# Order of the DMA transposes of q and k for two batches, in a fused sliding-window attention and GEGLU kernel

## The chip, the cores and the metric

The kernel runs on one core of a Trainium2 chip. The metric is the device time of one execution in microseconds (us). The kernel before has a median of 341.93 us over 3 runs (341.65 to 343.43). TensorE is called PE, VectorE DVE, ScalarE ACT, GpSimd POOL and SyncE SP. SP computes nothing here: it issues DMAs.

## The reference

Eight batches of attention with 8 heads, 576 positions and head size 64. Each query sees the 128 positions up to and including itself, with a bias that falls with distance (ALiBi). The result, as 4608 rows of 512, goes through a gated feed-forward block.

```python
scores = scale * np.matmul(q, k.transpose(0, 1, 3, 2))
mask = (rel >= 0) & (rel < window)                  # window = 128
scores = np.where(mask, scores + bias[None], -1000000000.0)
attn = softmax(scores)
x = np.matmul(attn, v)                              # heads side by side: 4608 x 512
out = (gelu(x @ w_gate) * (x @ w_val)) @ w_out      # 512 -> 1536 -> 512
```

## The kernel before

The work is written out by hand: the order of the instructions in the source is the order on each engine, and the framework adds only the semaphores. The outer loop `for g in range(NG)` (L909) runs over nine groups of 512 rows. Each group does the feed-forward block of its rows (`gate_val`, L597, with matmuls at L612; `out_part`, L641, with matmuls at L648) and, in between, pieces of the attention of a later batch. The list `todo` (L886) and the function `steps` (L891) say which pieces: in group 0, the scores of batch 1 and its products with v; in group 1, the scores of batch 2 ("s"), its products ("pv+"), and the scores of batch 3 ("s2"); in group 2, the products of batch 3 ("pv") and the scores of batch 4, and so on.

From batch 2 on, q and k of a batch come in like this. GpSimd issues ten loads, five of q and then five of k (`load_qk`, L112), which also turn float32 into bfloat16; five of v follow (`load_v`, L116). They land in buffers `qs`, `ks`, `vb`, two of each, used by even and odd batches in turn. Then `transposes_dma` (L169) makes SP issue six DMA transposes: one for all of k, into `kT` (L170), and five for q, one per block of 128 rows, into `qT` (L174). The scores need both: the matmuls at L206 (batches 0 to 2) and at L288 (from batch 3 on, `scores2`).

An engine takes its instructions in order, and an instruction that waits for a semaphore holds all that stand behind it. On SP the transposes stand in one line with the stores of the output (L638) and with small relays (L199), by which in `scores2` one row group of matmuls lets another begin. For batches 1 and 2 the relays of the products are on DVE instead. The transposes of batch 2 stand in the list of group 0; those of the later batches are issued when the next group starts (L910).

When GpSimd may start the loads of a later batch is ruled by marks: tiny copies on GpSimd that read an element which some earlier step writes, so that GpSimd waits for it. The mark at L952, at the end of group 0, reads `kT[0]`, so it waits for the k transpose of batch 2; then come the loads of q and k of batch 3 and of v of batch 2. The mark at L914, at the start of group 1, reads columns 128 and 129 of `qT[1]`, so it waits for the second q transpose of batch 3; then come the loads of q and k of batch 4 and of v of batch 3. The later marks (L936) read a result of the feed-forward block.

From batch 3 on the row sums are inverted and spread over the partitions by DMAs that ACT issues (`gather`, L435, and `spread_dma`, L443, with L445 filling `rb`), and DVE multiplies the products by them (L547). For batch 2 ACT does the inversion itself (L520, L521) and DVE multiplies at L524. ACT and DVE also copy the output from PSUM (L653), and ACT makes exp (L219) and gelu (L618). [...] a matmul can also wait for a bank to be read out.

Of the kernel before, what the change touches and what calls it, by code (L numbers as in the profile page):

```python
# [30 lines left out]
def kernel(  # L31
# [10 lines left out]
    nc = tc.nc  # L42
# [27 lines left out]
    def keep_busy(ps, n, w=64):  # L70
        for _ in range(n):
# [18 lines left out]
    mark = consts.tile([1, 2], BF16, name="mark")  # L90

    qs, ks = ([consts.tile([128, 5, DM], BF16, name=f"{nm}s{i}") for i in range(2)]
              for nm in "qk")
    qT, kT = ([consts.tile([128, 4, 640], BF16, name=f"{nm}T{i}") for i in range(2)]
              for nm in "qk")
# [16 lines left out]
    def load_qk(b):  # L112
        load(qs[b % 2], q, b)
        load(ks[b % 2], k, b)

    def load_v(b, js=range(5)):  # L116
        load(vb[b % 2], v, b, js, 64)
# [44 lines left out]
    def transpose(b, what, c, copy):  # L162
        ps = bank().bitcast(BF16)
        for n, lo in ((0, 0), (1, 384)):
            transpose_runs(b, n, what, c, ps[:, lo:576])
        for n, lo in ((0, 0), (1, 384)):
            untangle(copy, b, n, what, c, c + 1, ps[:, lo:576])

    def transposes_dma(b):  # L169
        nc.sync.dma_start_transpose(  # L170
            out=kT[b % 2].rearrange("p c (j t) -> p (c j) t", t=128),
            in_=ks[b % 2].rearrange("p j x -> p (j x)"))
        for j in range(5):
            nc.sync.dma_start_transpose(  # L174
                out=qT[b % 2][:, :, 128 * j:128 * j + 128], in_=qs[b % 2][:, j, :])


    Ps = [consts.tile([128, H, 896], BF16, name=f"P{i}") for i in range(2)]
# [188 lines left out]
    def add(b, c0, copy=None, what=(0, 1)):  # L367
        hs = slice(2 * c0, 2 * c0 + 4)
        P = Ps[b % 2].rearrange("p h (n y) -> p h n y", y=64)[:, hs]
        to = T.rearrange("p h (n y) -> p h n y", y=64)[:, hs]  # L370
        if 0 in what:
            for x in (0, 1):
                half = slice(64 * x, 64 * x + 64)
                nc.vector.tensor_tensor(  # L374
                    out=to[half, :, x:x + 7:2], in0=P[half, :, 0:10:3], in1=P[half, :, 1:11:3],
                    op=ALU.add)
            nc.vector.tensor_copy(out=to[0:64, :, 8], in_=P[0:64, :, 12])
            nc.vector.tensor_tensor(
                out=to[64:128, :, 8], in0=P[64:128, :, 11], in1=P[64:128, :, 12], op=ALU.add)
        if 1 in what:  # L380
            for x in (0, 1):
                half, n = slice(64 * x, 64 * x + 64), 4 - x
                (copy or nc.vector.tensor_copy)(
                    out=to[half, :, x + 1:x + 2 * n:2], in_=P[half, :, 2:3 * n:3])
# [30 lines left out]
    def sums4(b):  # L415
        ps = bank()
        for s, at in ((0, 0), (1, shape(b, 0)[1])):
            first, w = shape(b, s)
            mms = []
            for h in range(H):  # L420
                for x in (0, 1):
                    t = first + w * x
                    g, a = 2 * x + h // 4, 32 * (h % 4)
                    mms.append((g, ones8[:, a:a + 32], T[:, h, t:t + w]))
            for n, (g, lhsT, rhs) in enumerate(in_turn(mms)):
                nc.tensor.matmul(  # L426
                    out=ps[32 * g:32 * g + 32, at:at + w], lhsT=lhsT, rhs=rhs,
                    start=n < 4 and s == 0, stop=True, skip_group_check=True)
        for s, at in ((0, 0), (1, shape(b, 0)[1])):
            first, w = shape(b, s)  # L430
            nc.vector.reciprocal(row(b)[:, first:first + w], ps[:, at:at + w])  # L431
# [165 lines left out]
    def gate_val(g, f, lo=0, hi=512, later=None):  # L597
        if g not in hid:
            hid[g] = h_pool.tile([128, NF, 512], BF16, name="hT")
        t0 = 512 * g % RING  # L600
        n = hi - lo

        if n > 256 or lo >= 384:
            pg, pv = bank()[:, 0:n], bank()[:, 0:n]
            order = [(w, ps, c, c == 0) for w, ps in ((wg, pg), (wv, pv)) for c in range(4)]
        else:
            ps = bank()
            pg, pv = ps[:, 0:n], ps[:, n:2 * n]
            order = [(w, ps, c, w is wg and c == 0)
                     for cs in ((0, 1), (2, 3)) for w, ps in ((wg, pg), (wv, pv)) for c in cs]  # L610
        for w, ps, c, begins in order:
            nc.tensor.matmul(  # L612
                out=ps, lhsT=w[:, c, 128 * f:128 * (f + 1)], rhs=xT[:, c, t0 + lo:t0 + hi],
                start=begins, stop=(c == 3), skip_group_check=n <= 256 and lo < 384)

        def act():
            gl = g_pool.tile([128, 512], BF16, name="gelu")
            nc.scalar.activation(out=gl[:, 0:n], in_=pg, func=AF.Gelu)  # L618
            nc.vector.tensor_tensor(out=hid[g][:, f, lo:hi], in0=pv, in1=gl[:, 0:n],  # L619
                                    op=ALU.mult)  # L620

        if later is None:
            act()
        else:
            later.append(act)
# [79 lines left out]
    for h in (0, 2, 4, 6):  # L705
        for w, src in ((0, q), (1, k)):
            (nc.scalar if w and h == 0 else nc.sync).dma_start(
                out=raw[w][h // 4].rearrange("p (h x) -> p h x", h=4)[:, h % 4:h % 4 + 2, :],
                in_=src[0][h:h + 2, 0:384, :].rearrange("h (p r) d -> p h (r d)", r=3))
# [42 lines left out]
    def masks_of_last_blocks(lo, hi):  # L752
        nc.vector.tensor_copy(out=emask[:, lo:hi, 192:384], in_=emask[:, lo:hi, 0:192])
        nc.vector.tensor_copy(out=emask[:, lo:hi, 384:512], in_=emask[:, lo:hi, 0:128])
        for x, at in ((0, 128), (1, 0)):
            half = slice(64 * x, 64 * x + 64)
            nc.vector.tensor_copy(out=emask[half, lo:hi, 512:576], in_=emask[half, lo:hi, at:at + 64])
# [63 lines left out]
    for step in zip(*(inverse_first(0, x, sums_a[x]) for x in (0, 1))):  # L821
        for do in step:
            do()
    dve(out=pairs1.rearrange("p x (h d) -> p h x d", d=64),
        in_=vb[1].rearrange("p j x -> p (j x)")[:, 0:1536].rearrange(
            "p (h x d) -> p h x d", h=H, x=3))
# [6 lines left out]
    masks, waiting = [], []  # L833
# [38 lines left out]
    for n in range(2):  # L872
        nc.gpsimd.dma_start(
            out=wo[:, 6 * n:6 * n + 6, :],
            in_=moe_w_out[768 * n:768 * n + 768, :].rearrange("(c p) f -> p c f", p=128))
# [4 lines left out]
    for t in (qs[0], ks[0]):  # L880
# [3 lines left out]

    acts = (act, act, act, act)
    todo = {  # L886
        0: [("table",), ("s", 1, 0, (0, 1)), ("o", 0, 0, 0), ("o", 0, 1, 0), ("s", 1, 0, (2, 3)), ("o", 0, 0, 1), ("s", 1, 1, (0, 1)), ("o", 0, 1, 1), ("s", 1, 1, (2, 3), masks), ("pv+", 1, 0), 4, ("pv+", 1, 1), ("transposes", 2), 4],
        1: [("table",), ("s", 2, 0, (0, 1)), 3, ("s", 2, 0, (2, 3)), 2, ("s", 2, 1, (0, 1)), 2, ("s", 2, 1, (2, 3), masks), ("pv+", 2, 0), 3, ("pv+", 2, 1), 1, 2, ("s2", 3, 0), ("add", 3, 0), 3, ("s2", 3, 2), ("add", 3, 2, None, (0,))],
    }

# [18 lines left out]
    for g in range(NG):  # L909
        if 1 <= g < B - 2:  # L910
            transposes_dma(3 if g == 1 else g + 2)
        if g == 1:

            nc.gpsimd.tensor_copy(out=mark, in_=qT[1][0:1, 0, 128:130])  # L914
            load_qk(4)
            load_v(3)
        for f in range(9 if g == 0 else 0, NF):
            gate_val(g, f)
            if g == 2 and f == 2:
                add(3, 2, act, (1,))  # L920
            if g == 0 and f == 10:
                masks_of_last_blocks(0, 8)
            if g == 0 and f in (9, 11):
                for c in (0, 1) if f == 9 else (2, 3):
                    for w in (0, 1):
                        transpose(1, w, c, (act, dve)[w])
            if 2 <= g < B - 1:
                if f == (4 if g == 2 else 3):
                    sums4(g + 1)
                if f == (6 if g == 2 else 5):  # L930
                    gather(g + 1)
                if f == (8 if g == 2 else 7):
                    spread_dma(g + 1)
                if f == 9 and g + 2 < B:

                    nc.gpsimd.tensor_copy(out=mark, in_=hid[g][0:1, f, 0:2])  # L936
                    if g + 3 < B:
                        load_qk(g + 3)
                    load_v(g + 2)
        if g == 0:  # L940
            nc.gpsimd.memset(Ps[0][:, :, 0:64], 0.0)
            for t in (qs[1], ks[1]):
                nc.gpsimd.memset(t[64:128, 4, :], 0.0)
        for item in steps(g):
            if isinstance(item, int):
                out_part(g, item)
            else:
                RUN[item[0]](*item[1:])
        store()
        if g == 0:  # L950

            nc.gpsimd.tensor_copy(out=mark, in_=kT[0][0:1, 0, 512:514])  # L952
            load_qk(3)
            load_v(2)

# [29 lines left out]
```

## Time and profile before

| What | Value |
|---|---|
| Median of 3 runs | 341.93 us (341.65 to 343.43) |
| Profiled execution: its own time | 342.81 us |
| Profiled execution: its span | 341.0 us |
| Granted TensorE clock, mean | 0.998 |
| SP issues batch 2's k transpose, then its five q transposes | from 58.91 for 3.18 us, from 62.14 for 6.61 us |
| SP issues batch 3's k transpose, then its five q transposes | from 80.35 for 4.00 us, from 84.40 for 7.29 us |
| Mark L952 runs | at 64.10 us |
| Mark L914 runs | at 89.81 us |
| First scores of batch 2, of batch 3 | at 79.09 us, at 93.58 us |

Times inside the execution are counted from the start of the span. The span is shorter than the execution's own time, which has start and end around it. The profile comes from one execution; the median comes from others. PE's records are of pipelined matmuls with modelled ends, so a gap on PE is what counts, not its busy time. A line number in the profile is that of the kernel before.

### The profile page before, as it was taken

How to read it: one execution, taken by the hardware profiler on the slowest of the kernel's cores; microseconds unless marked ns; L12 is line 12 of the kernel's file. 1: busy time of each engine (PE TensorE's matmuls, PEld its weight loads, DVE VectorE, ACT ScalarE, POOL GpSimd, SP SyncE). 2: the span in 40 equal slices, each digit the busy share in tenths (PEclk: the TensorE clock that was granted, in tenths of full speed). 3: DMA queues.
4: the chain of work that ended last, by engine and by line, in shares of the span. 5: the costliest groups of instructions: out<-in, count | busy, mean ns of one | idle time of the engine just before them, and what ended most of it. 6: DMA issues, size and time to landing. Idle time of an engine off the chain costs nothing.

```text
span 341.0 us, 8148 instructions
## 1 busy us (share of the span) xinstructions
PE 329.0 (96%) x3299; PEld 169.9 (50%) x3342; DVE 192.5 (56%) x358; ACT 172.3 (51%) x321; POOL 106.4 (31%) x142
## 2 busy tenths in 40 slices
PE   8999999999979999999999999999999999999996
PEld 6667555444544454445544454445444544444443
DVE  7888766445659547943695369635974323303320
ACT  7974597438878328433763357344823133223321
POOL 6975763481481086007700680040000000000000
PEclk9999999999999999999999999999999999999999
DMA  8999999999999799949993999399106110020002
GB/s 211 169 193 191 204 164 146 139 184 163 98 207 187 108 173 189 199 110 152 178 190 81 163 179 195 73 161 111 63 3 140 63 62 1 2 93 31 2 31 92
DMA packets 150026, 43.49 MB, mean 128 GB/s; under 512 B 133572, under 2 KB 142948, under 8 KB 149988
## 3 DMA queue, kind: packets, MB, share of 16 engines
q0 software_dynamic: 107424, 18.10, 69.9%
q1 hardware_dynamic: 39104, 18.55, 22.9%
q10 hardware_dynamic: 3460, 6.32, 8.7%
q8 instruction: 26, 0.43, 0.5%
q14 instruction: 12, 0.10, 0.1%
HBM read 43.65 MB, written 9.53 MB: 156 GB/s over the span
## 4 chain that ended last, share of the span: by engine, by line
PE 71%; DMA 16%; POOL 4%; SPq 3%; DVE 2%; issue 2%; ACT 0%; ACTq 0%; DVEq 0%; POOLq 0%
PE ps L612 44%; PE ps L648 20%; DMA ks<-in_k_dram 6%; DMA wo<-in_moe_w_out_dram 5%; DMA rb<-rd 3%; PE ps L490 3%; PE ps L288 2%; POOL qs L108 2%; POOL ks L108 2%; SPq L174 2%; DMA qT<-qs 2%; DMA kT<-ks 2%; SPq L170 1%; PE ps L426 1%; PE ps L682 1%
## 5 line engine op out<-in xcount | busy, mean ns | idle before, releaser
L619 DVE TENSOR_TENSOR hT<-ps,gelu 128x512 bf16<-128x512 f32 (+3 forms) x119 | 73.9, 636 | 93.0 <-PE ps L612 85.3
L618 ACT ACTIVATE gelu<-ps 128x512 bf16<-128x512 f32 (+3 forms) x119 | 65.4, 558 | 101.1 <-PE ps L612 96.8
L612 PE MATMUL ps<-xT,wv 128*128 128x512 bf16 (+3 forms) x472 | 112.9, 359 | 0.5 <-DMA wv<-in_moe_w_val_dram 0.2
L612 PE MATMUL ps<-xT,wg 128*128 128x512 bf16 (+3 forms) x461 | 111.9, 359 | 1.1 <-issue 0.4
L648 PE MATMUL ps<-wo,hT 128*128 128x512 bf16 x375 | 87.8, 379 | 2.0 <-issue 1.1
L612 PEld LDWEIGHTS <-wv 128*128 128x128 bf16 x476 | 45.3, 98 | 49.2 <-issue 0.5
L612 PEld LDWEIGHTS <-wg 128*128 128x128 bf16 x476 | 44.7, 98 | 48.0 <-issue 0.3
L648 PEld LDWEIGHTS <-hT 128*128 128x128 bf16 x396 | 37.0, 98 | 43.8
L219 ACT ACTIVATE P<-ps 128x512 bf16<-128x512 f32 (+1 forms) x108 | 51.3, 578 | 4.5 <-PE ps L288 2.9
L222 DVE TENSOR_TENSOR P<-P,emask 128x768 bf16<-128x768 bf16 x60 | 31.3, 556 | 19.7 <-ACT P L219 18.0
L653 ACT COPY osb<-ps 128x512 f32<-128x512 f32 x28 | 16.4, 587 | 50.8 <-PE ps L648 50.8
L108 POOL DMA_DIRECT2D vb<-in_v_dram x40 | 33.9, 872 | 8.6 <-DMA qs<-in_q_dram 2.5
L108 POOL DMA_DIRECT2D qs<-in_q_dram x30 | 25.3, 861 | 6.0 <-DMA wo<-in_moe_w_out_dram 4.2
L936 POOL COPY mark<-hT 1x2 bf16<-1x2 bf16 x4 | 0.7, 176 | 81.4 <-DVE hT L619 81.4
L108 POOL DMA_DIRECT2D ks<-in_k_dram x30 | 25.4, 887 | 0.3 <-DMA qs<-in_q_dram 0.3
L547 DVE TENSOR_TENSOR xT<-ps,rb 128x512 bf16<-128x512 f32 (+3 forms) x34 | 14.6, 501 | 7.2 <-PE ps L490 4.8
L490 PE MATMUL ps<-P,vb 64*64 64x192 bf16 (+2 forms) x752 | 16.9, 220 | 0.2
L490 PEld LDWEIGHTS <-vb 64*64 64x64 bf16 x752 | 14.4, 107 | 3.1 <-issue 2.6
L374 DVE TENSOR_TENSOR T<-P 64x1024 bf16<-64x1024 bf16 x20 | 13.7, 686 | 0.6
L288 PE MATMUL ps<-qT,kT 64*64 64x192 bf16 (+2 forms) x440 | 9.6, 224 | 2.5 <-DMA qT<-qs 1.9
L288 PEld LDWEIGHTS <-kT 64*64 64x64 bf16 x440 | 7.6, 107 | 7.4 <-issue 7.2
L431 DVE RECIPROCAL r<-ps 128x128 f32<-128x128 f32 (+1 forms) x10 | 9.8, 1021 | 0.0
(92 smaller groups left out, 184.3 us busy)
## 6 DMA issues: line engine op xcount, KB each, us to landing
out_dram<-osb SPq DMA_DIRECT2D x35, 256.0 KB
rb<-rd ACTq DMA_DIRECT2D x10, 576.0 KB
vb<-in_v_dram POOLq DMA_DIRECT2D x32, 128.0 KB, 6.8
qs<-in_q_dram POOLq DMA_DIRECT2D x24, 128.0 KB, 5.7
ks<-in_k_dram POOLq DMA_DIRECT2D x24, 128.0 KB, 6.9
wo<-in_moe_w_out_dram POOLq DMA_DIRECT2D x2, 768.0 KB, 14.7
wg<-in_moe_w_gate_dram POOLq DMA_DIRECT2D x5, 256.0 KB, 8.5
wv<-in_moe_w_val_dram POOLq DMA_DIRECT2D x5, 256.0 KB, 9.1
```

What stands on the lines that cost most here:

```text
L108: nc.gpsimd.dma_start(out=t[at:at + n, j, :].rearrange("p (h d) -> p h d", h=H), in_=src[b][:, 128 * j:128 * j + n, :].rearrange("h p d -> ...
L219: nc.scalar.activation(out=dst, in_=src, func=AF.Exp, scale=0.125)
L222: nc.vector.tensor_tensor(out=dst, in0=dst, in1=m, op=ALU.mult)
L288: mm = nc.tensor.matmul(out=ps[64 * x:64 * x + 64, col:col + w], lhsT=keys(b, c, m)[half, :], rhs=qT[b % 2][half, c, q0:q0 + w], start=Tru ...
L374: nc.vector.tensor_tensor(out=to[half, :, x:x + 7:2], in0=P[half, :, 0:10:3], in1=P[half, :, 1:11:3], op=ALU.add)
L490: mm = nc.tensor.matmul(out=out, lhsT=lhsT, rhs=prob(b)[half, c, i, col:col + q1 - q0], start=all(t[2] != u for t in todo[:n]), stop=True, ...
L547: nc.vector.tensor_tensor(out=xT[:, c, at:at + e - a], in0=src, in1=recip[b][:, c, a:e], op=ALU.mult)
L612: nc.tensor.matmul(out=ps, lhsT=w[:, c, 128 * f:128 * (f + 1)], rhs=xT[:, c, t0 + lo:t0 + hi], start=begins, stop=(c == 3), skip_group_che ...
L618: nc.scalar.activation(out=gl[:, 0:n], in_=pg, func=AF.Gelu)
L619: nc.vector.tensor_tensor(out=hid[g][:, f, lo:hi], in0=pv, in1=gl[:, 0:n], op=ALU.mult)
L648: nc.tensor.matmul(out=acc[g], lhsT=hid[g][:, f, 128 * t:128 * (t + 1)], rhs=wo[:, f, :], start=(f == 0), stop=(f == NF - 1))
L653: (nc.vector.tensor_copy if g < B - 2 and t in by_dve.get(g, (0,)) else nc.scalar.copy)(out=osb, in_=acc[g])
```

## The change

Three edits. First, `transposes_dma` issues the five q transposes ahead of the k transpose for batches 2 and 3; from batch 4 on the order stays k, then q. Second, the entry of batch 2's transposes in the list of group 0 stands ahead of the second half of batch 1's products instead of behind it. Third, the two marks read other elements: that of L952 the last block of `qT[0]`, which the last of the five q transposes of batch 2 writes; that of L914 a column of `kT[1]`, which the k transpose of batch 3, now the last of six, writes.

```diff
     def transposes_dma(b):
-        nc.sync.dma_start_transpose(
-            out=kT[b % 2].rearrange("p c (j t) -> p (c j) t", t=128),
-            in_=ks[b % 2].rearrange("p j x -> p (j x)"))
+        def of_k():
+            nc.sync.dma_start_transpose(
+                out=kT[b % 2].rearrange("p c (j t) -> p (c j) t", t=128),
+                in_=ks[b % 2].rearrange("p j x -> p (j x)"))
+
+        if b > 3:
+            of_k()
         for j in range(5):
             nc.sync.dma_start_transpose(
                 out=qT[b % 2][:, :, 128 * j:128 * j + 128], in_=qs[b % 2][:, j, :])
+        if b <= 3:
+            of_k()
...
-        0: [... ("pv+", 1, 0), 4, ("pv+", 1, 1), ("transposes", 2), 4],
+        0: [... ("pv+", 1, 0), 4, ("transposes", 2), ("pv+", 1, 1), 4],
...
         if g == 1:
 
-            nc.gpsimd.tensor_copy(out=mark, in_=qT[1][0:1, 0, 128:130])
+            nc.gpsimd.tensor_copy(out=mark, in_=kT[1][0:1, 0, 512:514])
             load_qk(4)
             load_v(3)
...
         if g == 0:
 
-            nc.gpsimd.tensor_copy(out=mark, in_=kT[0][0:1, 0, 512:514])
+            nc.gpsimd.tensor_copy(out=mark, in_=qT[0][0:1, 0, 512:514])
             load_qk(3)
             load_v(2)
```

More of the change, by code (lines that the diff above doesn't have):

```diff
@@ L886 @@
     todo = {
-        0: [("table",), ("s", 1, 0, (0, 1)), ("o", 0, 0, 0), ("o", 0, 1, 0), ("s", 1, 0, (2, 3)), ("o", 0, 0, 1), ("s", 1, 1, (0, 1)), ("o", 0, 1, 1), ("s", 1, 1, (2, 3), masks), ("pv+", 1, 0), 4, ("pv+", 1, 1), ("transposes", 2), 4],
+        0: [("table",), ("s", 1, 0, (0, 1)), ("o", 0, 0, 0), ("o", 0, 1, 0), ("s", 1, 0, (2, 3)), ("o", 0, 0, 1), ("s", 1, 1, (0, 1)), ("o", 0, 1, 1), ("s", 1, 1, (2, 3), masks), ("pv+", 1, 0), 4, ("transposes", 2), ("pv+", 1, 1), 4],
         1: [("table",), ("s", 2, 0, (0, 1)), 3, ("s", 2, 0, (2, 3)), 2, ("s", 2, 1, (0, 1)), 2, ("s", 2, 1, (2, 3), masks), ("pv+", 2, 0), 3, ("pv+", 2, 1), 1, 2, ("s2", 3, 0), ("add", 3, 0), 3, ("s2", 3, 2), ("add", 3, 2, None, (0,))],
```

## The prediction

> **What bounds the kernel now.** I read the page's first two parts, the list of waits of PE, the chain of waits that ended last, the timeline around PE's longest gap, and the DMA queues slice by slice.
>
> ```profile
> PE 329.0 (96%) x3299; PEld 169.9 (50%) x3342; DVE 192.5 (56%) x358; ACT 172.3 (51%) x321; POOL 106.4 (31%) x142
> ```
>
> TensorE (PE) is busy 329.0 of 341.0 us at a granted clock of 0.998. Only its gaps, 12 us in all, can be won. PE's waits, longest first (total, times, longest):
>
> ```profile
> PE ps L288 <- DMA qT<-qs: 1.9, 1, 1.9
> PE ps L648 <- issue: 1.1, 7, 0.2
> PE ps L72 <- DVE zeros L696: 1.0, 1, 1.0
> PE ps L288 <- DVE xT L547: 0.6, 2, 0.3
> ```
>
> Two concern the change. The longest is the scores of batch 3 (L288) waiting for a transposed q. The 0.6 is a later wait for the DVE multiply L547, which itself waited for a DMA (rb<-rd). The chain of waits shows where both come from (start, length, what):
>
> ```profile
> 52.24 6.47 DMA ks<-in_k_dram
> ...
> 58.91 5.14 DMA kT<-ks
> ...
> 64.10 0.18 POOL mark L952
> ...
> 71.96 8.18 DMA ks<-in_k_dram
> ...
> 80.35 4.00 SPq L170
> ...
> 84.40 1.26 SPq L174
> ...
> 87.08 1.99 SPq L174
> ...
> 90.48 5.24 DMA qT<-qs
> ...
> 95.76 0.81 PE ps L288 x27
> ...
> 115.66 0.66 ACTq L445
> ...
> 116.36 10.36 DMA rb<-rd
> ...
> 126.84 2.49 DVE xT L547 x4
> ```
>
> Read downwards: batch 2's k lands at 58.7, its transpose lands at 64.05 and lets mark L952 go; batch 3's loads start; its k lands at 80.19; SP issues the k transpose (4.00) and only then five q transposes (7.29 with the gaps), though q had landed long before; the last q lands at 95.72. PE had been ready since 93.58:
>
> ```profile
> 91.79 2.65 SPq L638 DMA_DIRECT2D out_dram<-osb  x3
> 92.98 1.55 DVE L524 TENSOR_TENSOR xT<-ps,rb 128x512 bf16<-128x512 f32 x3
> 93.38 0.57 ACT L653 COPY osb<-ps 128x512 f32<-128x512 f32 x1
> 93.58 0.28 PE L288 MATMUL ps<-qT,kT 64*64 64x64 bf16 x4
> 95.76 0.84 PE L288 MATMUL ps<-qT,kT 64*64 64x192 bf16 x40 [1.90 <-DMA qT<-qs]
> ```
>
> What loads and transposes do to each other is seen in the queues (q0: GpSimd's loads, q1: SP's stores and transposes; packets, MB, share). First pair: half a microsecond from 67.0, both at work. Then loads alone, 78 to 80, and transposes alone, 61 to 62.
>
> ```profile
> q0 software_dynamic: 212, 0.03, 82.3%
> q1 hardware_dynamic: 203, 0.05, 78.7%
> ...
> q0 software_dynamic: 2445, 0.31, 241.5%
> ...
> q1 hardware_dynamic: 839, 0.21, 117.1%
> ```
>
> Alone, loads move some 611 packets per half microsecond and transposes 420; together 212 and 203.
>
> [...] So a transpose that waits at the head of SP's stream holds all behind it, as the 24.6 us that SP spent at L170 waiting for k show. [...]
>
> **The change, part by part.**
>
> *Batch 2's entry moved up* past ("pv+", 1, 1). Nothing that this entry issues goes to SP (its relays are on DVE, its stores are issued by the output parts), so on SP, PE, ACT, DVE and GpSimd every instruction keeps its place. 0 us.
>
> *Batch 2, q ahead of k.* The five q transposes no longer stand behind the wait for k (58.91). SP is free from its second store at 50.2; the last q load was issued at 48.09 and its kind lands in 6.0 (54.1). At 1.26 us each they are issued by about 56.6 instead of 68.75. Their packets now meet k's loads. From 66.5 to 72.5 three transposes met loads: 3985 load packets where 6 us at 1222 allow 7335, so 2.75 us lost, 0.9 per transpose. At most some two of the five find k's backlog still there: k lands at about 60.5 instead of 58.74, its transpose 5.14 later, about 66. First use: scores at 79.09, covered by feed-forward matmuls of 20 us. Cover left 13 us, cost 0. The stores behind (68.85) go out earlier, near 65.
>
> *First mark (L952)* now waits for the last q instead of k. Issue ends at 56.6; the last q of batch 3, under load, took 5.24 more. So about 61.8 instead of 64.10 (59.5 if loads hinder little, 64 if much).
>
> *Batch 3, q ahead of k.* From mark to k landed took 16.1 us. Now all five q transposes fall in that stretch where three did: 2 x 0.9 more, and k's transpose of batch 2 overlaps its start, 0.6 more. k lands at 61.8 + 16.1 + 2.4 = 80.3, as before. Only k's transpose is then missing. Batch 2's took 5.14 with 3.18 of issue; with the 4.00 of issue seen here, 6.0. kT lands near 86.3, 7 us ahead of PE's 93.58. The five q transposes (7.3 us of SP) are off the path. The wait goes.
>
> *What is late next.* The 44 matmuls of that step take 0.87 undisturbed. They also need banks from L524 (last needed about 94.2) and L653 (93.95), some 0.1; and their relay stands on SP behind the store of that L653 copy, some 0.45 after 93.95, where PE arrives at about 94.25: 0.3. So they end at 93.58 + 0.87 + 0.35 = 94.8 instead of 96.60: **1.8 us** gained (2.15 if nothing of this shows, 1.4 if the relay costs twice that). The v loads of batch 2 stand behind the same transposes: issued at 72.67 they landed 8.3 later (81.0), the last at 84.1; needed at 85.83 and 89.3. A delay of 2.4 fits into the 4 us of cover.
>
> *Second mark (L914)* now waits for kT, the last of six, instead of the second q: 86.4 instead of 89.81. Behind it on GpSimd stand batch 4's loads and v of batch 3, and on their landing (106.2) SP's transposes of batch 4. These start 3.4 earlier, against a PE 1.8 earlier: 1.6 to the good, more because the loads no longer meet q transposes (at 92 to 94 only 258 load packets passed). That matters for rb: from 116 to 120, with batch 4's transposes still in flight, its queue moved 58 packets; in the next batch, undisturbed, 447 in 152 to 156. With transposes out of the way rb lands before DVE has anything to scale, and the 0.6 goes: **0.5 us** taken, bounds 0 and 0.6.
>
> Sum: 1.8 + 0.5 = **2.3 us**. The profiled execution took 342.81 (span 341.0 and 1.8 around it); it becomes 340.5. It lay 0.9 above the median of 341.93, so the median becomes **339.6**. A measurement of this kernel can tell about 0.5%, 1.7 us, from no change.
>
> **The rivals.** *Half gain:* the first wait goes, but relay and banks cost 0.7 and rb doesn't move: 1.4 us, 340.5. For it: SP is issuing a store just then. Against: only one store is left to issue. Also here: v late by more than its 4 us of cover, each microsecond beyond costs one. Within 0.5%.
>
> *Slower:* q transposes and loads get in each other's way far more than 0.9 us each. For it: at 92 to 94 both together passed 71 GB/s against 154 for loads alone. k of batch 3 then lands late, kT with it, and the second mark waits for kT: the price falls due at rb. Batch 4's transposes are level with PE, compared with now, if kT lands at 89.7 (16.4 us less the 1.7 lost at 92 to 94 after the mark, 1.8 for PE); each microsecond later delays rb by one. At 91.5 the gain is eaten, beyond it the kernel is slower. With 1.4 us per q transpose more than reckoned, 7 in all, kT lands at 93.3 and the kernel takes 341.93 - 1.8 + 3.6 = 343.7.
>
> *It doesn't do what it says:* k's landing, not q's place, sets the end anyway. Then PE waits for kT in place of qT. Against: k landed at 80.19, 13.4 us ahead of PE, and its transpose needs 6.
>
> **How the numbers follow.** Main case 0.68 (own range 339.1 to 340.2), half gain 0.24 (340.2 to 341.9), slower 0.08. From these: faster by over 0.5% 0.68, within 0.5% 0.24, slower 0.08. The range runs from 338.9, both waits gone whole and a quiet run, to 341.3, which takes in most of the half gain.
>
> **What would show it.** Right: in PE's waits qT<-qs is gone or under 0.5; SP's L174-kind transposes of batch 2 start near 50 and those of batch 3 near 70, before k lands; the marks run near 62 and 86; the wait for L547 is gone; the step of L288 near 93.6 lasts 1.2. Wrong: k of batch 3 landing after 84, a wait of PE for kT or vb, or the second mark later than 89.8.

## The result, and the profile after

| What | Before | After | Predicted for after |
|---|---|---|---|
| Median, runs of one comparison (14 each) | 343.25 us (341.36 to 346.53) | 339.72 us (339.17 to 341.19) | 339.6 (338.9 to 341.3) |
| Ratio after to before, 95% interval | | 0.9899 (0.9868 to 0.9931) | |
| Profiled execution, its own time | 342.81 us | 339.51 us | 340.5 |
| Its span, its granted clock | 341.0 us, 0.998 | 337.7 us, 1.000 | |

The kernel became faster by about 1%. The ratios, here and below, leave out executions more than 1.5% above the fastest of the same kernel; medians and ranges keep them. Line numbers of the kernel after are 6 or so higher: L288, L547 and L648 of before are L294, L553 and L654, and the two transposes L170 and L174 are L171 and L178.

PE's busy time in the page after, then its list of waits (total, times, longest):

```profile
PE 331.6 (98%) x3342; PEld 169.7 (50%) x3342; DVE 192.3 (57%) x358; ACT 172.0 (51%) x321; POOL 106.6 (32%) x142
```

```profile
PE ps L72 <- DVE zeros L702: 1.0, 1, 1.0
PE ps L771 <- DVE ks L753: 0.5, 1, 0.5
PE ps L496 <- DVE P L228: 0.3, 1, 0.3
PE ps L771 <- DVE qs L753: 0.2, 1, 0.2
```

Both waits that the prediction named are gone: none for `qT` or `kT`, none for L553, which multiplies by `rb`. (The busy time of before, 329.0, came from 3299 records of the same 3342 matmuls, so its difference says nothing, and the prediction's 12 us of gaps, taken from it, are too many.)

SP's instructions after, in order of time (start, length, what):

```profile
50.12 8.62 SPq L178 DMA_TRANSPOSE qT<-qs  x5
63.09 3.25 SPq L171 DMA_TRANSPOSE kT<-ks  x1
...
69.30 8.91 SPq L178 DMA_TRANSPOSE qT<-qs  x5
82.63 4.41 SPq L171 DMA_TRANSPOSE kT<-ks  x1
```

Batch 2's q transposes now start at 50.12, batch 3's at 69.30, each some 13 us ahead of the transpose of k, which alone is left when k has landed. GpSimd's two marks after (in brackets how long it stood and for what):

```profile
63.79 0.18 POOL L958 COPY mark<-qT 1x2 bf16<-1x2 bf16 x1 [9.55 <-DMA qT<-qs]
...
90.69 0.18 POOL L920 COPY mark<-kT 1x2 bf16<-1x2 bf16 x1 [11.11 <-DMA kT<-ks]
```

The second one dates the landing of `kT`: 90.65, where the prediction had 86.3, and still 2.8 us ahead of PE. PE's timeline after, at batch 3's scores:

```profile
91.38 2.12 PE L654 MATMUL ps<-wo,hT 128*128 128x512 bf16 x9
93.43 1.25 PE L294 MATMUL ps<-qT,kT 64*64 64x64 bf16 x44
94.61 2.12 PE L654 MATMUL ps<-wo,hT 128*128 128x512 bf16 x9
```

From its start to the next group the step lasts 94.61 - 93.43 = 1.18; before, the last score ended at 95.76 + 0.84 = 96.60 (the matmul behind it has no record), so the step lasted 96.60 - 93.58 = 3.02. That is 1.84 less; 1.8 was predicted. The second place is batch 4's first scores. PE's timeline before, then after:

```profile
127.87 0.61 PE L288 MATMUL ps<-qT,kT 64*64 64x64 bf16 x16
128.78 0.27 PE L288 MATMUL ps<-qT,kT 64*64 64x192 bf16 x2 [0.29 <-DVE xT L547]
129.38 0.64 PE L288 MATMUL ps<-qT,kT 64*64 64x192 bf16 x26 [0.33 <-DVE xT L547]
129.96 1.25 PE L648 MATMUL ps<-wo,hT 128*128 128x512 bf16 x4
```

```profile
125.85 0.87 PE L294 MATMUL ps<-qT,kT 64*64 64x64 bf16 x44
126.65 2.76 PE L654 MATMUL ps<-wo,hT 128*128 128x512 bf16 x12
```

129.96 - 127.87 = 2.09 became 126.65 - 125.85 = 0.80: 1.29 less. The list of waits of before showed only 0.29 + 0.33 of it, because it counts a gap from the modelled end of a matmul, and modelled ends reach into the gap. So in this pair of executions the two places gave 1.84 + 1.29 = 3.1 of the 3.3 us by which the two profiled executions differ (342.81 - 339.51).

### The profile page after: what moved, and what is told of

Read it like the earlier page. It is cut to its first block, busy times and chain, and to the rows that moved or that the text cites. A ratio compares the mean times of both kernels' runs of the same rounds, so it can differ in the third digit from the quotient of the medians.

```text
span 337.7 us, 8194 instructions
## 1 busy us (share of the span) xinstructions
PE 331.6 (98%) x3342; PEld 169.7 (50%) x3342; DVE 192.3 (57%) x358; ACT 172.0 (51%) x321; POOL 106.6 (32%) x142
## 4 chain that ended last, share of the span: by engine, by line
PE 91%; ACT 4%; DVE 1%; DMA 1%; issue 1%; SPq 1%; DVEq 0%
PE ps L618 55%; PE ps L654 25%; PE ps L496 4%; PE ps L294 2%; ACT P L225 2%; PE ps L674 2%; PE ps L212 1%; DMA ks<-in_k_dram 1%; PE ps L432 1%; PE ps L688 1%; PE ps L150 1%; ACT rb L572 1%; SPq L713 1%; ACT rb L571 0%; DVE xT L530 0%
## 5 line engine op out<-in xcount | busy, mean ns | idle before, releaser
L625 DVE TENSOR_TENSOR hT<-ps,gelu 128x512 bf16<-128x512 f32 (+3 forms) x119 | 73.9, 637 | 93.0 <-PE ps L618 86.3
L618 PE MATMUL ps<-xT,wg 128*128 128x512 bf16 (+3 forms) x476 | 113.5, 359 | 0.2
L654 PE MATMUL ps<-wo,hT 128*128 128x512 bf16 x396 | 90.3, 380 | 0.0
L654 PEld LDWEIGHTS <-hT 128*128 128x128 bf16 x396 | 37.1, 98 | 43.6
L228 DVE TENSOR_TENSOR P<-P,emask 128x768 bf16<-128x768 bf16 x60 | 31.3, 556 | 18.6 <-ACT P L225 16.9
L553 DVE TENSOR_TENSOR xT<-ps,rb 128x512 bf16<-128x512 f32 (+3 forms) x34 | 14.7, 502 | 5.5 <-PE ps L496 5.5
L294 PEld LDWEIGHTS <-kT 64*64 64x64 bf16 x440 | 7.6, 107 | 4.4 <-issue 4.2
```

What stands on the lines that cost most here:

```text
L228: nc.vector.tensor_tensor(out=dst, in0=dst, in1=m, op=ALU.mult)
L294: mm = nc.tensor.matmul(out=ps[64 * x:64 * x + 64, col:col + w], lhsT=keys(b, c, m)[half, :], rhs=qT[b % 2][half, c, q0:q0 + w], start=Tru ...
L553: nc.vector.tensor_tensor(out=xT[:, c, at:at + e - a], in0=src, in1=recip[b][:, c, a:e], op=ALU.mult)
L618: nc.tensor.matmul(out=ps, lhsT=w[:, c, 128 * f:128 * (f + 1)], rhs=xT[:, c, t0 + lo:t0 + hi], start=begins, stop=(c == 3), skip_group_che ...
L654: nc.tensor.matmul(out=acc[g], lhsT=hid[g][:, f, 128 * t:128 * (t + 1)], rhs=wo[:, f, :], start=(f == 0), stop=(f == NF - 1))
```

## The experiments

**The parts of the change.** The changed kernel again (after_again), beside the executions of before that the later runs shared.

> The changed kernel itself once more, beside the same executions of the kernel before as the other runs of this group, so that they can be compared with it directly. Expected by all theories: 339.2 to 341.2 with a median near 339.7, the granted clock 0.998 or more in over nine tenths of the executions, and a ratio to the kernel before of 0.989 to 0.995.

Measured: 339.83 us (339.42 to 341.17, 7 runs), ratio 0.9912 (0.9877 to 0.9948), the clock at 0.998 or more in all seven. As expected.

Only batch 3 with q first (b3_alone); batch 2 in the old order, the first mark as before:

```diff
-        if b > 3:
+        if not (b == 3):
             of_k()
...
-        if b <= 3:
+        if b == 3:
             of_k()
...
-            nc.gpsimd.tensor_copy(out=mark, in_=qT[0][0:1, 0, 512:514])
+            nc.gpsimd.tensor_copy(out=mark, in_=kT[0][0:1, 0, 512:514])
```

> Only batch 3 has q ahead of k; batch 2 and its mark as in the kernel before. Theory (batch 3's order is the change): PE's wait for qT is gone, the step of batch 3's scores lasts about 1.2 us where it lasted 3.0, and the time is that of the changed kernel, 339.7 within 0.5. Rival (both batches are needed, because batch 2's order brings the first mark forward): PE waits at least 1 us for kT or qT and the time lies between the two kernels, 341 to 342.

Measured: 340.17 us (339.46 to 341.26, 6 runs), ratio 0.9899 (0.9863 to 0.9934). Its waits of PE, in the profiled execution of 341.26:

```profile
PE ps L294 <- DVE xT L553: 0.8, 3, 0.3
PE ps L496 <- issue: 0.5, 1, 0.5
```

No wait for `qT` or `kT`: batch 3's order alone removes it, and the time is the theory's, 339.7 within 0.5. Batch 3's first step of scores lasts 1.09. Here `rb` was late (10.77 us from issue to landing), and there is a new stop of 0.5 us that waits for nothing the profile shows; more on it below.

Only batch 2 with q first (b2_alone); batch 3 in the old order, the second mark as before:

```diff
-        if b > 3:
+        if not (b == 2):
             of_k()
...
-        if b <= 3:
+        if b == 2:
             of_k()
...
-            nc.gpsimd.tensor_copy(out=mark, in_=kT[1][0:1, 0, 512:514])
+            nc.gpsimd.tensor_copy(out=mark, in_=qT[1][0:1, 0, 128:130])
```

> Only batch 2 has q ahead of k, and the first mark waits for its last q; batch 3 and the second mark as in the kernel before. Theory (batch 3's order is the change): the wait for qT stays at 1.5 to 3 us, the time is within 0.3% of the kernel before. Rival (an earlier first mark brings all that follows forward): batch 3's k lands 2 us earlier than 80.2, the wait is gone, and the time comes down by 1.5 us or more.

Measured: 340.9 us (339.52 to 346.06, 8 runs), ratio 0.9929 (0.9894 to 0.9964). In the profiled execution (340.4) SP began batch 3's k transpose at 79.27 instead of 80.35 and its q transposes at 83.28 instead of 84.40, and PE waited for neither. The first mark came no earlier (64.20, before 64.10), but the loads behind it met no q transposes of batch 2 any more: from the mark to SP's k transpose of batch 3 it took 15.1 us instead of 16.3. So the old order of batch 3, a single microsecond earlier, can be enough in some executions; that its times reach up to 346.06 suggests that in others it isn't. Neither theory was fully right, and batch 2's part has an effect, where the prediction gave it none.

The old order, with the second mark on the last q instead of the second (late_mark_alone):

```diff
-            nc.gpsimd.tensor_copy(out=mark, in_=qT[1][0:1, 0, 128:130])
+            nc.gpsimd.tensor_copy(out=mark, in_=qT[1][0:1, 0, 512:514])
```

> The kernel before with one edit: the second mark waits for the last q transpose of batch 3 instead of the second, so batch 4's loads can't meet the last q transposes. Theory (batch 3's q stands last in line, and that is the wait): PE still waits over 0.7 us for qT, since five transposes of 1.26 us stand behind k's; time down by at most 1 us. Rival (the loads that the mark lets go stretch the landing of the last q from 2 to 5.2 us, and that is the wait): the last q lands near 92.5, the wait is under 0.3, time down by 1.5 us or more.

Measured: 342.19 us (339.39 to 346.48, 22 runs), ratio 0.9970 (0.9946 to 0.9993). Its longest wait of PE after the start:

```profile
PE ps L288 <- DMA qT<-qs: 1.0, 1, 1.0
```

The last q transpose took 4.20 us from the start of its issue to its landing (91.29 to 95.50), where before it took 5.24 (90.48 to 95.72). So the loads behind the mark stretched it by about 1 us, not by the rival's 3.2, and the theory holds. PE came later in this execution (94.26 for 93.58), which is most of why the wait is 1.0 and not 1.9. Keeping the loads away, without the order, brings 0.3%.

The changed kernel with the second mark where it was, on the second q (early_mark):

```diff
-            nc.gpsimd.tensor_copy(out=mark, in_=kT[1][0:1, 0, 512:514])
+            nc.gpsimd.tensor_copy(out=mark, in_=qT[1][0:1, 0, 128:130])
```

> The changed kernel, but the second mark reads the second q transpose of batch 3 as it did before, not the k transpose, which is the last of six. The q transposes now come first, so this mark is passed near 77 to 80 instead of 90.7 and the loads of batch 4 run while batch 3's k is transposed. Theory A (the mark is what keeps the new order's gain: loads beside the transpose stretch it): kT lands some 1 to 3 us later than 90.65, so at 92 to 94 against TensorE's need at 93.4; a wait of 0 to 0.6 us comes back and the time is 339.7 to 340.4, nothing gained. Theory B (earlier loads free batch 4's transposes and with them rb): rb lands earlier, no wait comes back, and the time is at or below 339.5 in all executions. Rival to both (the loads crowd out the transpose altogether): kT lands after 95.5 and the time is back above 341.

Measured: 345.08 us (343.63 to 346.33, 6 runs), ratio 1.0104 (1.0061 to 1.0147): slower than before. The time is the rival's, but none of the three had the reason. `kT` was there when PE came to it at 95.17. PE stood still twice, for nothing that the profile shows:

```profile
90.94 0.36 PE L496 MATMUL ps<-P,ones 64*64 64x128 bf16 x4
92.66 0.53 PE L496 MATMUL ps<-P,vb 64*64 64x128 bf16 x20 [1.36 <-issue]
...
98.08 0.87 PE L294 MATMUL ps<-qT,kT 64*64 64x64 bf16 x44
98.89 0.39 PE L618 MATMUL ps<-xT,wg 128*128 128x512 bf16 x1
102.40 1.06 PE L618 MATMUL ps<-xT,wg 128*128 128x512 bf16 x2 [3.12 <-issue]
```

The clock then fell too, as the stretches of that kernel's execution show (PEclk is the last figure but two):

```profile
102.00:104.00 2.00, 1.60 (x4) 0.68 (x5) 1.96 (x5) 1.92 (x3) 0.00 (x0) 0.54 2.21 194
104.00:108.00 4.00, 4.00 (x16) 1.67 (x15) 3.83 (x8) 0.69 (x2) 0.00 (x0) 0.80 1.54 171
```

1.36 + 3.12 and 2 x 0.46 + 4 x 0.20 = 1.7 of lost clock make 6.2, all of the 6.1 by which the spans differ (343.8 to after's 337.7).

A new theory: PE ran out of instructions. Every kernel's page lists a queue of its own for them (packets, MB, share):

```profile
q8 instruction: 26, 0.43, 0.5%
```

The 26 packets hold 0.43 MB, 16.5 KB each. Over the 3342 matmuls and as many weight loads of the kernel after they would be one for every 257 instructions, an estimate that gives all of q8 to PE. early_mark's q8 packets begin at 90.23 and 99.52, and PE goes on 2.4 and 2.9 after these. In the kernel after they begin at 88.33 and 92.60. The theory: loads and transposes at once (832 and 831 packets in 88 to 90 in early_mark) hold up these packets too. The stops would then belong to places in PE's stream, not to what stands there. 64 tiny matmuls at the start, added to early_mark, shift the stream (early_mark_shift):

```diff
     keep_busy(held[0], 60)
+    keep_busy(held[0], 64, 2)
```

> The changed kernel with the second mark on the second q transpose (as in early_mark), and 64 more matmuls of 2 columns at the start of the program, which put every later TensorE instruction 128 places further down its stream (each matmul is a weight load and a matmul). In early_mark TensorE stood still for 1.36 us inside batch 2's products and for 3.12 us right after batch 3's scores, waiting for nothing that the profile shows. Theory (TensorE ran out of instructions[...]): the two stops move to other places of the program, 64 matmuls earlier[...], and the time stays over 342. Rival (TensorE waits for a bank, a semaphore or vb that the profile doesn't name): the stops stay before the same matmuls, the 30th or so of the ones and P products and the second of group 1's first gate block, with about the same lengths.

Measured: 342.06 us (341.11 to 344.76, 14 runs), ratio 0.9985 (0.9957 to 1.0012). PE's timeline there:

```profile
95.55 0.89 PE L294 MATMUL ps<-qT,kT 64*64 64x64 bf16 x34 [0.32 <-ACT osb L659]
97.34 0.39 PE L294 MATMUL ps<-qT,kT 64*64 64x192 bf16 x10 [0.90 <-issue]
97.66 2.12 PE L654 MATMUL ps<-wo,hT 128*128 128x512 bf16 x9
99.71 0.87 PE L294 MATMUL ps<-qT,kT 64*64 64x64 bf16 x44
```

The stop inside batch 2's products is gone, and the other stands after 34 of the first 44 scores. From there to early_mark's place are 10 + 9 + 44 + 1 = 64 matmuls, exactly the shift; its q8 packet begins at 94.69, 2.7 before PE goes on. The theory holds, and the rival (a bank, a semaphore, `vb`) falls. Counted in PE's weight loads, early_mark's two stops come after 1253 and 1383 of them, 130 apart: with their matmuls 260 instructions, close to the estimate's 257. The time fell by 3 us although there was more to do. The 0.5 stop of b3_alone is at the same place as early_mark's first (behind the same four products with ones; packet at 89.06, PE goes on at 91.48). The kernel after passes that place at about 90.85 with its packet at 88.33, 2.5 earlier: it just gets by. PE passed the place 128 weight loads earlier in the stream, about a packet back by the estimate, at 86.1 to 86.3 in before, after and early_mark alike, but the packet began 0.5 us later than that in before, 2.2 in after and 3.9 in early_mark. The last two differ in batch 4's early loads, so that share goes to them; what delays the packet in after isn't shown. So the third edit, the mark on the last of the six, is what keeps the new order's gain.

**Whose order?** The mirror image: the transposes in the old order, k's loads of batches 2 and 3 first, the marks on the last q (k_loads_first; the marks' lines are left out):

```diff
-        load(qs[b % 2], q, b)
-        load(ks[b % 2], k, b)
+        for t, src in ((ks, k), (qs, q)) if b < 4 else ((qs, q), (ks, k)):
+            load(t[b % 2], src, b)
```

> The mirror image of the change: the transposes keep the order of the kernel before, k then q, but GpSimd issues k's loads of batches 2 and 3 ahead of q's, and the two marks wait for the last q transpose. Theory (what matters is that SP's order is the order in which the loads land, so that only one short transpose is left when the last load has landed): TensorE waits for neither kT nor qT at batch 3, the last q lands before 92, and the time is 339.3 to 340.5, like the changed kernel. Rival (it is k's one long transpose, which has to be the last, or the q transposes, which have to start early, that brings the gain): a wait of over 1 us for qT stays, and the time is 341 or more.

Measured: 339.8 us (339.28 to 341.69, 22 runs), ratio 0.9943 (0.9924 to 0.9962). Its second mark, now on the last q:

```profile
90.85 0.17 POOL L914 COPY mark<-qT 1x2 bf16<-1x2 bf16 x1 [11.34 <-DMA qT<-qs]
```

The last transpose lands at about the same time as after (90.69), and PE waits for none. The theory holds. So neither q nor k has to be first: what counts is that SP's order is the order of landing.

The changed kernel with q first for batches 4 to 7 too (q_first_all; `of_k()` always behind the loop):

> The changed kernel with q ahead of k for the later batches 4 to 7 too. Theory (the order only matters where the last transpose lands after TensorE needs it; from batch 4 on all six land some 8 us or more ahead, and they are queued when all loads have landed or nearly so): within 0.5 us of the changed kernel, 339.3 to 340.3. Rival (rb or the stores of those groups feel the order): it differs by more than 0.7 us, in either direction.

Measured: 340.33 us (339.35 to 341.92, 22 runs), ratio 0.9942 (0.9921 to 0.9963); 0.5 over after_again, at the edge of what was expected, with the executions spread wider. Its profile has the same 0.55 stop for instructions as b3_alone; that stands at 91.4, ahead of all that this edit changes. Its `rb` was late too, so that batch 4's first step of scores lasted 1.50 instead of 0.80: the DMA ahead of it (rd) took 5.1 us, while batch 4's k transpose, now last, was issued beside it. Nothing gained; whether a little is lost stays open.

**rb.** The kernel before without batch 4's six transposes (no_t4_before); its scores then use batch 2's:

```diff
-        if 1 <= g < B - 2:
+        if 1 <= g < B - 2 and g != 2:
             transposes_dma(3 if g == 1 else g + 2)
```

> The kernel before without batch 4's six DMA transposes; its scores then read what batch 2 left in kT and qT. Theory (rb is late because batch 4's transposes are in flight with it): rb lands within 7.5 us of its issue instead of 10.4, DVE's wait for rb is gone, batch 4's first step of scores lasts 0.9 instead of 2.15, and the time comes down by about 1.2 us; the wait for qT stays. Rival (rb is slow by itself, or because of batch 5's loads): rb still takes 9 us or more, DVE still waits, time as before.

Measured: 343.94 us (340.18 to 346.54, 22 runs), ratio 1.0011 (0.9982 to 1.0040). The wait for L547 went, as expected, but `rb` took 8.8 us from issue to landing, between the theory's 7.5 and the rival's 9, and the time stayed. The profile showed why the time stayed: after the wait for qT (2.08 us, to 95.81) PE's clock fell. Its activity by the microsecond (stretch, length, busy time and instructions of PE, PEld, DVE, ACT and POOL, then PEclk, DMA share, GB/s):

```profile
95.00:96.00 1.00, 0.19 (x13) 0.19 (x16) 0.00 (x0) 0.00 (x0) 1.00 (x2) 1.00 1.67 228
96.00:97.00 1.00, 0.84 (x41) 0.72 (x34) 0.00 (x0) 0.77 (x2) 1.00 (x2) 0.91 2.28 161
97.00:98.00 1.00, 1.00 (x3) 0.30 (x2) 0.65 (x2) 1.00 (x3) 0.55 (x1) 0.50 1.72 268
98.00:99.00 1.00, 1.00 (x4) 0.39 (x3) 0.39 (x1) 1.00 (x3) 0.63 (x1) 0.50 2.15 176
99.00:100.00 1.00, 1.00 (x4) 0.22 (x2) 0.69 (x2) 0.28 (x1) 0.97 (x3) 0.50 2.35 166
100.00:101.00 1.00, 1.00 (x45) 0.69 (x44) 0.90 (x2) 0.58 (x2) 0.85 (x1) 0.88 2.40 160
```

The lost clock is 0.09 + 3 x 0.50 + 0.12 = 1.7 us. In 13 of this kernel's 22 executions the mean clock was 0.995 or less (median 344.65), in 9 it was 0.998 or more (341.55, only 0.2 below before's 341.78 at that clock). The same split runs through the executions of before that stood beside all these runs: 75 of 156 at 0.995 or less (343.91), 81 above (341.78).

The kernel after without batch 4's transposes (no_t4_after; the same edit):

> The changed kernel without the six DMA transposes of batch 4; the scores of batch 4 read what batch 2 left in the same buffers. Theory (what is left of the spread among the changed kernel's executions, 339.2 to 341.2, is rb of batch 3, which has to share the DMA engines with batch 4's transposes): all executions lie within 339.2 to 340.0, rb lands within 8 us of its issue, and DVE's multiply of batch 3 waits for no DMA. Rival (the spread comes from elsewhere, or rb is late on its own account): some executions stay at 341, and the median moves by less than 0.2 from 339.7.

Measured: 340.0 us (339.21 to 341.7, 22 runs), ratio 0.9942 (0.9924 to 0.9961). In its profile DVE's multiply waits for no DMA, but it doesn't in the profile of the kernel after either, and the median didn't fall. All but two lie under 340.7, those two at a clock of 0.994 and 0.993. `rb` can't be more than a part of after's spread; the theory's "all within 340.0" missed.

Do batch 4's transposes make `rb` late? From issue to landing it took 10.4 us in before and 8.8 without them, but 8.6 in after and 9.0 without them, and 8.5 in fill_gap, the next run, where before's transposes are all in place and batch 4's first step of scores lasts 0.80. So the profiles don't show that they are the cause; it stays open.

**The clock.** The kernel before, with 38 idle matmuls in front of batch 3's first scores (fill_gap), then with 24 (fill_short):

```diff
         for key in ((c0, 0), (c0 + 1, 1), (c0 + 1, 0)):
             own[key] = bank()
+        if (b, c0) == (3, 0):
+            keep_busy(own[c0, 1], 38, 128)
```

> The kernel before, with 38 idle matmuls of 128 columns (about 2.1 us of TensorE work whose result nobody reads) ahead of batch 3's first scores; the transposes keep their order, k then q. So TensorE still can't use the scores' operands before 95.7, but doesn't stand still while they come. Theory (the long pause of TensorE sometimes costs it half of its clock for some 3.4 us after it, 1.7 us, on top of the wait itself): the granted clock is 0.998 or more in nearly all executions, where it was in about half of the kernel before's; the median falls to about 341.5 from about 343.1, though the wait itself, now filled, is as long as before. Rival (the lower clock comes from elsewhere, such as the start or the load as a whole): about half of the executions still have 0.995 and take 343 to 344, and the median stays within 0.5 of the kernel before.

Measured: 341.99 us (341.08 to 343.67, 22 runs), ratio 0.9999 (0.9979 to 1.0019); the clock at 0.998 or more in all 22, where before had 31 of 59 beside it. The median fell by only 0.45 (342.44 for before beside it), so the rival had the time right, the theory the clock. The pause is filled:

```profile
93.88 2.29 PE L72 MATMUL ps<-zeros 128*128 128x128 bf16 x38
96.10 0.87 PE L290 MATMUL ps<-qT,kT 64*64 64x64 bf16 x44
```

> The kernel before with 24 idle matmuls of 128 columns (about 1.3 us) ahead of batch 3's first scores, where fill_gap had 38 (2.1 us): TensorE's pause ahead of those scores is not filled, only shortened, from some 2.1 to some 0.8 us, and the scores start when qT lands. Theory (the pause has to be long for the clock to fall[...]): the granted clock is 0.998 or more in nearly all executions, and the median is about 341.5, half a microsecond below fill_gap's 341.99. Rival (any pause there may cost the clock): 0.995 comes back in over a quarter of the executions.

Measured: 341.77 us (340.52 to 347.3, 22 runs), ratio 0.9975 (0.9950 to 1.0000); the clock at 0.998 or more in 19 of 22. The three below are fewer than the rival's quarter and more than none. Its profiled execution, the fastest of the 22, has no pause left at all; how long the pauses of the others were isn't shown.

The clock theory holds: the pause costs the clock, in about half of the executions (75 of before's 156 at 0.995 or less; with the pause filled, none of 22). The time didn't come down as far as expected; a likely reason is that the idle matmuls always take their time (96.10 - 93.88 = 2.2 us in the profile), also where qT would have been there sooner. Filling the pause only steadies the kernel; removing it also saves it.

## Why the prediction came out right, point by point

- **Batch 3's order, 1.8 us:** right, 1.8 measured in the profiled pair. b3_alone shows that this edit does it, k_loads_first that the mechanism is the order of landing, late_mark_alone that a later mark by itself isn't enough.
- **Batch 2's edits, 0 us:** wrong as "0". b2_alone, at a ratio of 0.9929, brought k of batch 3 about a microsecond earlier and was enough in some executions. The moved entry was not tried alone.
- **Mark L952 at 61.8, kT at 86.3, mark L914 at 86.4:** all too early. They came at 63.79, 90.65 and 90.69. The price of "0.9 per transpose" held. k of batch 2 landed at 63.0 instead of 58.7, though its loads were issued 0.3 earlier: 4.6 us for five transposes, 0.9 each; and from the mark to k of batch 3 it took 18.6 us, reckoned 16.1 + 2.4. Three other terms failed. "At most some two of the five" were to meet k's loads (k at 60.5), but all five were issued before k had landed. The issue of batch 2's five q transposes took 8.6 us instead of 6.3 ("1.26 us each"), which put the first mark 2.0 late. (The 5.24 added there counts from the start of an issue, not from its end.) And batch 3's k transpose took 8.0 (82.63 to 90.65) instead of 6.0, which put `kT` another 2.0 late. Batch 2's v loads landed until 86.65 beside it; whether they stretched it, no run shows. By the prediction's own list of what would show it wrong, the second mark (90.69, limit 89.8) is on the wrong side. The 7 us of cover had shrunk to 2.8, and it held.
- **rb, 0.5 us:** the wait went, but its size was off, 1.29 in the profiled pair. It was bounded by 0.6 from the list of waits, although the same working corrected the first wait from 1.90 to 2.15 by comparing the step's length with an undisturbed 0.87. The same correction here gives 2.09 - 0.80. The reason given, batch 4's transposes out of rb's way, isn't borne out: with them `rb` took 8.6 us in after, without them 9.0. That this wait went in the profiled execution may be luck.
- **"Each later microsecond of kT delays rb by one":** not borne out. `kT` landed later than the level of 89.7, batch 4's six transposes were issued from 105.69 to 117.83 (before: 106.21 to 116.91), and still `rb` came in time, though by 0.1 us only (landed at 122.96; DVE's multiply at 123.08 waited only for PE). In b3_alone, with the second mark 0.7 later, it came late. What decides it from execution to execution stays open.
- **The level:** 340.5 less the 0.9 by which the profiled execution lay above a median of three runs. In larger groups before's median is 342.4 to 343.3, so that execution was no outlier. The 0.9 stood in for what was missing from the sum, 3.3 for 2.3. The time was hit partly because two errors offset each other.
- **The clock:** not priced at all. Among executions at 0.998 or more before has 341.78, and after_again has 339.83: 1.95 for the waits alone, not 3.1, so they aren't always as long as in the profiled execution. The mixture with 75 of 156 executions that lose another 2.1 (343.91 - 341.78) adds about 1.
- **The rival "slower":** its direction was real, its place wrong. Loads beside the transposes can lose more than the change wins (early_mark, at a ratio of 1.0104), not by kT or rb but by late instructions for PE, in stops of 1.36 and 3.12 us.

## What to carry to other kernels

Queue DMAs behind one issuing engine in the order in which what they wait for arrives, and judge what is left by the last landing against the consumer's start: here 90.65 against 93.43, at a ratio of 0.9899. When an order brings transfers forward, move the marks that release the next loads with it: in early_mark the loads let in early cost more than the order gains (345.08 us, where after_again has 339.83). Size a stall by the length of the whole step against an undisturbed one, not by the wait list.

## What the runs showed of the hardware

- After a stop of PE of 2.08 us (no_t4_before) the clock was 0.91, 0.50 three times and 0.88 in the next five microseconds: 1.7 us lost, or half a clock for about 3.4 us (1.7 / 0.50). After early_mark's stop of 3.12 it was 0.54 over two microseconds and 0.80 over four, 1.7 us lost as well. In the profiled execution of before a stop of 1.90 left the clock at 1.00 in each microsecond from 92 to 100. Why it held there and fell after the 2.08 isn't shown.
- PE's stops in early_mark fit instructions that come late by DMA, in q8's packets (26, 0.43 MB): with 64 matmuls added at the start a stop came 64 matmuls earlier in the program (early_mark_shift). With loads and transposes at once (832 and 831 packets in 88 to 90 in early_mark) PE stood still for up to 3.12 us and went on 2.4 and 2.9 us after a packet began. In the kernel after the packet began 2.5 us before PE came to the place of the first stop, and PE didn't stop there.
- Loads with DMA transposes beside them landed later: with five q transposes beside its loads, batch 2's k landed at 63.0 (after) instead of 58.7 (before), its loads issued 0.3 earlier. That is 4.6 us, 0.9 each.
